# Attention and experts: the router's logits of two tiles at a time taken up later, key and weight transfers asked for one tile sooner

## The chip, the cores and the metric

The kernel runs on one core of a Trainium2 chip. The metric is device time in microseconds (us) from the first to the last instruction of one launch, lower being better; the median of several runs stands for a kernel.

The engines are named as the profile names them: PE is TensorE (matmuls and transposes; PEld are its weight loads, which overlap), DVE is VectorE, ACT is ScalarE, POOL is GpSimd, and SP is the engine from which nearly all transfers (DMAs) are issued. Each engine runs its own list of instructions in order and waits on semaphores for the others.

## The reference

Attention over 4 batches, 8 heads, 768 positions and 64 channels: each query sees the 96 latest positions and 8 global ones. The result is the input of a mixture of 8 experts, each of which takes at most 80 of the tokens whose best logit is its own.

```python
def _attn_ref(q, k, v, n_global, n_local):
    scores = scale * np.matmul(q, k.transpose(0, 1, 3, 2))
    is_global = pos[None, :] < int(n_global)
    is_local = (rel >= 0) & (rel < int(n_local))
    scores = scores - slopes[:, None, None] * dist[None, :, :]
    scores = np.where(is_global | is_local, scores, -1000000000.0)
    a = np.exp(scores - np.max(scores, axis=-1, keepdims=True))
    a = a / (np.sum(a, axis=-1, keepdims=True) + 1e-09)
    return np.matmul(a, v)

def _moe_ref(x, w_gate, w1, w2, capacity):
    logits = x @ w_gate                                   # 3072 x 8
    expert_idx = np.argmax(logits, axis=1)
    gate_w = softmax(logits)[np.arange(N), expert_idx]
    for e in range(E):
        tok_idx = np.where(expert_idx == e)[0]            # the 80 of largest gate_w
        h = np.maximum(x[tok_idx] @ w1[e], 0.0)           # 512 -> 1024
        out[tok_idx] = gate_w[tok_idx, None] * (h @ w2[e])
```

## The kernel before

The 3072 queries are 24 tiles of 128. A tile is two units, u = 2t and 2t + 1, of four heads each; 48 units in all. The main loop (L391 to L424) runs over units and is a software pipeline. In unit u stand, in this order:

- `scores(u)`: PE multiplies queries and keys into PSUM (L181); DVE adds the bias table and takes the row's extreme (L201); ACT takes the exponential and its sum (L205). Between its halves come `transposes(u - 2)`, in which PE turns the weights of two units ago (L242, L250; from u = 20 also a finished tile on its way to DRAM, L255) and ACT copies half of the result to SBUF (L259), and `invert` and `norm` of unit u - 1 (DVE L213, L214; POOL L222).
- `logits2` in every fourth unit: PE transposes the router's logits of two tiles (L330), and DVE reduces them (L359).
- `copied(u - 2)`: DVE copies the other half of the turned weights (L265); from u = 20 the transfer of a finished quarter to `x_dram` (L268) is issued here.
- `logits1` in every fourth unit: PE multiplies two finished tiles by the gate matrix (L318), and DVE copies the product to SBUF (L322).
- `weigh(u - 3)`: PE multiplies weights and values into the one PSUM buffer `pair` (L289, L298). After the second unit of a tile ACT copies `pair` out (L312), and the next tile's first L289 must wait for that copy.
- in even units, SP is asked for the queries of tile u/2 + 2 (`load_q`, 256 KB) and for the next block of keys (`next(keys)`, 272 KB); in odd units for the values of tile u//2 + 1 (two transfers, 208 and 256 KB) and for what `ASKS` names: w is a quarter of an expert's weights (512 KB), o a wipe of a part of the output.
- `routes(n)`: n steps of a generator that finds, group by group (tiles 0 to 5, 6 to 11, 12 to 17, 18 to 21, 22 and 23), each token's expert and gate: small instructions on DVE, POOL and ACT (L505 to L511), comparisons against 127 thresholds (`cf`, L545, DVE), their count by expert on PE (L601), and the rest (L561 onwards; L581 to L588 on POOL). A step may be empty.

The order of PE, DVE, ACT, POOL and SP is the order in which the program is written. Unit 47 and what is left of the pipeline are written out by hand in the string `DRAIN` (L58): its letter r is one routing step, a1 and a2 are `logits1` and `logits2` of tiles 20 and 21, n47 is the last `norm`, t45 to t47 and w44 to w47 are what is left of transposes and weighing. Then a search for each expert's threshold runs, and then the experts' matmuls (L843). A transfer on SP takes one of eight semaphores in turn; a ninth waits until the oldest has landed.

Of the kernel before, what the change touches and what calls it, by code (L numbers as in the profile page):

```python
# [24 lines left out]
NT = B * NB  # L25
# [22 lines left out]
MASK = -8.0e9 * 64  # L48

EARLY = "k12 q1 v0 k23 v1 q2 w0"  # L50
ASKS = "- - w w w w w w w w - o - w - o - w - - w - - -".split()
HELD, EVERY, AHEAD, LATE = 2, 3, 14, 2
FROM, INSIDE = 18, 14
HOLD = 20


DRAIN = (
# [14 lines left out]
def fast_path(tc, a, out, cst, x_dram, inp):  # L72
# [4 lines left out]
    with ExitStack() as ctx:  # L77
# [63 lines left out]
        with tc.tile_pool(name="at_sb", bufs=2) as sp, ExitStack() as sctx:  # L141
# [8 lines left out]
            def idle(n):  # L150
                wake = cst["svx"].rearrange("p s t -> p (s t)")
                for _ in range(n):
                    T.matmul(lps[:, :480], wake[:, :P], wake, start=True, stop=True, skip_group_check=True)

            def begin(u):
                st[u] = [
                    sp.tile([P, 4], F32, tag="nm", bufs=3, name=f"nm{u}"), sp.tile([P, 4], F32, tag="z", bufs=3, name=f"z{u}"),
                    sp.tile([P, 4, WH], F32, tag="ts", name=f"ts{u}"), pwz[u % 3][:, :4 * WH].rearrange("p (j k) -> p j k", j=4),
                ]
# [102 lines left out]
            def copied(u):  # L262
                spot = u - FROM
                ta, tp, n = st[u, "ta"]
                (A.copy if u == nu - 2 else V.tensor_copy)(out=ta[:, 1, :n], in_=tp[:, :n])  # L265
                if 0 <= spot < 2 * INSIDE:
                    r = TURN[spot // 2] * P
                    nc.sync.dma_start(  # L268
                        out=x_dram[r:r + P, :].rearrange("p (i g c) -> p i g c", i=2, g=2)[:, :, spot % 2], in_=ta[:, :, n - P:n])
                st[u, "ta"] = ta  # L270
# [45 lines left out]
            def logits1(t, n):  # L316
                for pr in range(NP):
                    T.matmul(  # L318
                        lps[32 * pr:32 * pr + 32, :n * P], cst["wgn"][:, pr, :], st[t, "ut"][:, pr, :n, :], start=True, stop=True,
                        skip_group_check=True)  # L320
                ls = sp.tile([P, n * P], F32, tag=f"ls{n}", name=f"ls{t}")
                (A.copy if t == NT - 2 else V.tensor_copy)(out=ls, in_=lps[:, :n * P])  # L322
                st[t, "l"] = ls

            def logits2(t, n):

                ls = st.pop((t, "l"))
                if n == 2:
                    for i in range(2):
                        T.transpose(out=part(t + i), in_=ls[:, P * i:P * i + P], identity=ident)  # L330
                else:
                    T.matmul(lgs(t), ls, cst["pick"], start=True, stop=True, skip_group_check=True)
                for i in range(n):
                    collect(t + i)

            def part(t):
                return lps[:, :P] if t % 2 else lps[:, 2 * P:3 * P]

            def lgs(t):
                if t == NT - 1:  # L340

                    if t not in st:
                        st[t] = psa.tile([P, 512], F32, tag="tp0", name="lgl")[:, :E]
                    return st[t]
                if t not in st:
                    st[t] = psa.tile([P, 512], F32, tag="tp1", name="lgk")[:, :E]
                return st[t]

            def collect(t):
                g = next(i for i in range(len(GROUPS)) if t < sum(GROUPS[:i + 1]))  # L350
                n, t0 = GROUPS[g], sum(GROUPS[:g])
                if t == t0:
                    st["rt"] = Route(nc, sp, cst, t0, n)
                rt = st["rt"]
                if n < 3:
                    rt.one(lgs(t), t - t0)
                else:
                    lp = part(t).rearrange("p (q k) -> p k q", q=NP)
                    V.tensor_reduce(out=rt.lg[:, t - t0, :], in_=lp[:, :E, :], axis=AX.X, op=ALU.add)  # L359
                    if t == t0 + n - 1:  # L360
                        routing.append(rt.all())
                        if t0 == 0:
                            routing.append(rt.scale(lps[:, P * NP - 1:]))
                if t == t0 + n - 1:
                    if t < NT - 1:
                        routing.append(rt.rest(lps[:, 3 * P:3 * P + E], cst["capm"]))
# [9 lines left out]
            def routes(n):  # L376
                for _ in range(n):
                    while routing and next(routing[0], END) is END:
                        routing.pop(0)

            routing, cst["later"], cst["landed"] = [], [], []
            nu = 2 * NT
            late = late_constants(nc, a, cst)
            keys = inp.keys(3)
# [6 lines left out]
            for u in range(nu - 1):  # L391
                if u == 0:
                    for _ in cst["first"]:
                        pass
                begin(u)
                scores(u)
                if u % 4 == 1 and 9 <= u:
                    logits2((u - 9) // 2, 2)
                if 2 <= u:
                    copied(u - 2)  # L400
                if u == 1:
                    for _ in window:
                        pass
                    for z in pwz:
                        G.memset(z[:, 4 * WH:], 0.0)
                    G.memset(cst["zero"], 0.0)
                if u > 2:
                    for _ in range(3):
                        next(late, None)
                if u % 4 == 0 and 8 <= u:  # L410
                    logits1((u - 8) // 2, 2)
                if 3 <= u:
                    idle(2 if u == 3 else 0)
                    weigh(u - 3)
                if u % 2 == 0 and 3 <= u // 2 + 2 < NT:
                    inp.load_q(u // 2 + 2, hold=u < HOLD)
                    for _ in range(1 + (u == 20)):
                        next(keys, None)
                if u % 2:
                    if 2 <= u // 2 + 1 < NT:  # L420
                        inp.load_v(u // 2 + 1, hold=u < HOLD)
                    for k in ASKS[u // 2]:
                        next(dict(w=ahead, o=wipe).get(k, iter(())), None)
                routes(5 if u > 40 else 2 + (u % 4 == 3))  # L424
            u = nu - 1
            begin(u)
            scores(u)
# [1 line left out]
            def whole(u):  # L429
                transposes(u)  # L430
                copied(u)

            step = dict(
                w=lambda: next(ahead), o=lambda: next(wipe), t45=lambda: copied(u - 2), t46=lambda: whole(u - 1), t47=lambda: whole(u),
# [957 lines left out]
def build(tc, a, out):  # L1392
    nc = tc.nc
    with tc.tile_pool(name="cst", bufs=1) as cp, tc.tile_pool(name="dr", bufs=1, space=DRAM) as dp:
        x_dram = dp.tile([B * S, DM], F32, name="x_dram")
        lg_dram = dp.tile([B, P, NB, E], F32, name="lg_dram")
        sg_dram = dp.tile([E, P, NT], F32, name="sg_dram")
        cst = Constants(nc, cp)
        late_tiles(cst)
        with tc.tile_pool(name="at_in", bufs=1) as ip:  # L1400
            early = tc.manual_schedule(engines=ORDERED)
            early.__enter__()
            inp = Inputs(nc, a, ip)

            for n, t in (("rel", inp.vb[0]), ("bias", inp.vb[3])):
                cst[n], cst[n + "w"] = t[:, :2 * WH].rearrange("p (h k) -> p h k", h=2), t
            for i, n in enumerate(("r0", "k0", "b0")):
                cst[n] = inp.kt[1].rearrange("p q k -> p (q k)")[:, P * i:P * i + (NG if n == "k0" else P)]
            constants(nc, a, cst)
            inp.more(cst)  # L1410
            early.__exit__(None, None, None)
            fast_path(tc, a, out, cst, x_dram, inp)
            sure = nc.values_load(cst["sure"], min_val=0, max_val=1)
            with tc.If(sure < 1):
                general_path(tc, a, out, cst, x_dram, lg_dram, sg_dram)
# [44 lines left out]
```

## Time and profile before

| | |
|---|---|
| time of three runs, median (lowest, highest) | 257.93 us (257.54, 258.23) |
| time of the profiled execution | 259.51 us |
| span of that execution, first to last instruction | 257.7 us |
| PE, DVE, ACT, POOL busy | 239.6, 213.7, 208.0, 107.5 us |
| granted TensorE clock, mean | 0.977 of full speed |

In the trace the attention takes the span up to 131 us, the drain 131 to 142, the search 142 to 155, the experts 155 to 255. A tile of the attention is told by the starts of its first scores on PE: unit 6 at 20.08 us, unit 8 at 25.16, and so on every 4.6 to 6.9 us; unit 46 starts at 128.04.

A row of the windows gives, for one stretch, its length and then the busy time of PE, PEld, DVE, ACT and POOL (with the number of instructions), the granted clock, the busy share of the 16 DMA engines, and GB/s. A row of a timeline gives start, length, engine, line, operation, output and inputs, the number of instructions run together, and in brackets the idle time before it and what ended that. Where the bracket says "issue", the engine waited for nothing that the profile shows.

### The profile page before, as it was taken

To read this page: it belongs to the slowest core of one execution; us is meant where nothing else is said; L and a number is where in the kernel's file an instruction comes from. 1 tells how busy PE (TensorE), PEld (TensorE's weight loads), DVE (VectorE), ACT (ScalarE), POOL (GpSimd) and SP (SyncE) were. 2 spreads that over 40 slices of the span, in tenths; PEclk is the share of its full clock that TensorE was granted. 3 is DMA by queue.
4 is the path that set the end of the run, shared out by engine and by line. 5 is a ranking of instruction groups with operands and counts; after the bars stand their busy time and mean duration, and the time that the engine had idled before them with its cause. 6 is when DMAs were issued, how large, how long until landed. Compare 5 with 4: busy or idle time off the path is not lost.

```text
span 257.7 us, 9711 instructions
## 1 busy us (share of the span) xinstructions
PE 239.6 (93%) x3587; PEld 169.2 (66%) x3587; DVE 213.7 (83%) x782; ACT 208.0 (81%) x584; POOL 107.5 (42%) x214
## 2 busy tenths in 40 slices
PE   7989998998899999999998798999999999999991
PEld 2567766766677777877667655666666666666660
DVE  3777778987779799898987778999999898999860
ACT  3889899998899999999886636887979898979740
POOL 7667674644445745457470638810000022221111
PEclk9999999999999999999999659999999999999998
DMA  5758999999998999988649976999999999999101
GB/s 145 235 159 218 330 287 280 282 304 300 274 301 247 287 284 316 319 251 230 216 138 311 384 265 204 347 333 401 404 410 408 407 397 398 389 405 364 51 25 36
DMA packets 49086, 73.06 MB, mean 284 GB/s; under 512 B 3688, under 2 KB 23528, under 8 KB 49032
## 3 DMA queue, kind: packets, MB, share of 16 engines
q1 hardware_dynamic: 47864, 69.74, 81.3%
q0 software_dynamic: 1024, 2.62, 3.2%
q8 instruction: 30, 0.49, 0.8%
q14 instruction: 24, 0.20, 0.3%
q10 hardware_dynamic: 144, 0.00, 0.0%
HBM read 58.46 MB, written 13.89 MB: 281 GB/s over the span
## 4 chain that ended last, share of the span: by engine, by line
PE 63%; ACT 13%; DVE 10%; DMA 4%; issue 4%; POOL 3%; SPq 0%; POOLq 0%; DVEq 0%; ACTq 0%
PE hp L843 17%; PE yp L843 17%; ACT pwz L205 9%; PE ring L181 6%; PE pair L289 5%; PE pair L298 3%; DMA kt<-in_kT_dram 3%; PE tp L242 3%; ACT ta L259 2%; DVE ts L201 2%; POOL pwz L222 2%; PE tp L898 2%; PE lps L318 1%; DMA q<-in_q_dram 1%; PE lps L330 1%
## 5 line engine op out<-in xcount | busy, mean ns | idle before, releaser
L205 ACT ACTIVATE pwz<-ts,nm 128x168 f32<-128x168 f32 (+1 forms) x192 | 81.5, 427 | 10.3 <-DVE z L213 6.0
L222 POOL TENSOR_TENSOR pwz<-pwz,z 128x672 f32<-128x672 f32 (+2 forms) x48 | 60.2, 1255 | 53.4 <-DVE z L214 35.5
L201 DVE CUSTOM_DVE_ANT_0 ts<-ring,tab 128x168 f32<-128x168 f32 (+1 forms) x192 | 53.2, 315 | 11.7 <-PE ring L181 11.0
L181 PE MATMUL ring<-kt,q 64*64 64x64 f32 (+3 forms) x1088 | 41.0, 275 | 1.0 <-DMA q<-in_q_dram 0.5
L926 POOL DMA_INDIRECT out_dram<-vb,si x8 | 10.0, 1248 | 76.3 <-ACT xt5h L836 37.9
L205 ACT ACTIVATION_READ_ACCUMULATOR pwz<-ts,nm 128x1 f32 x192 | 36.5, 190 | 0.0
L181 PEld LDWEIGHTS ring<-kt,q 64*64 64x64 f32 x1088 | 32.5, 137 | 4.7 <-issue 2.2
L289 PE MATMUL pair<-ta,va 104*64 104x128 f32 (+1 forms) x368 | 30.5, 285 | 5.1 <-ACT ut L312 3.5
L289 PEld LDWEIGHTS pair<-ta,va 104*64 104x64 f32 (+1 forms) x368 | 19.3, 136 | 14.1 <-issue 7.1
L265 DVE COPY ta<-tp 128x512 f32<-128x512 f32 (+2 forms) x46 | 28.3, 616 | 0.0
L259 ACT COPY ta<-tp 128x512 f32<-128x512 f32 (+2 forms) x47 | 23.8, 507 | 0.5 <-ACT pwz L205 0.5
L242 PE MATMUL tp<-ident,pwz 64*128 64x64 f32 x376 | 21.7, 235 | 1.4 <-POOL pwz L222 0.5
L242 PEld LDWEIGHTS tp<-ident,pwz 64*128 64x128 f32 x376 | 15.3, 138 | 9.1 <-POOL pwz L222 3.5
L817 DVE TENSOR_TENSOR w_3l<-w,w_3h 128x1024 fp32r<-128x1024 f32 x16 | 19.6, 1223 | 1.4 <-ACT w_3h L813 1.3
L817 DVE TENSOR_TENSOR w_0l<-w,w_0h 128x1024 fp32r<-128x1024 f32 x15 | 18.3, 1222 | 2.0 <-ACT w_0h L813 2.0
L298 PE MATMUL pair<-ta,vb 64*64 64x64 f32 x640 | 18.7, 231 | 0.0
L817 DVE TENSOR_TENSOR w_1l<-w,w_1h 128x1024 fp32r<-128x1024 f32 x15 | 18.3, 1220 | 0.0
L817 DVE TENSOR_TENSOR w_2l<-w,w_2h 128x1024 fp32r<-128x1024 f32 x15 | 18.3, 1218 | 0.0
L298 PEld LDWEIGHTS pair<-ta,vb 64*64 64x64 f32 x640 | 13.2, 133 | 6.8 <-issue 6.7
L813 ACT CAST w_3h<-w 128x1024 fp32r<-128x1024 f32 x16 | 16.7, 1045 | 0.3 <-PE yp L843 0.3
L813 ACT CAST w_2h<-w 128x1024 fp32r<-128x1024 f32 x15 | 15.9, 1058 | 1.2 <-PE hp L843 1.0
L201 DVE DVE_READ_ACCUMULATOR2_ANT nm<- 128x1 f32 x192 | 16.0, 83 | 0.0
(441 smaller groups left out, 525.9 us busy)
## 6 DMA issues: line engine op xcount, KB each, us to landing
w<-in_w_dram SPq DMA_DIRECT2D x64, 512.0 KB
kt<-in_kT_dram SPq DMA_DIRECT2D x23, 272.0 KB
out_dram<-zero SPq DMA_DIRECT2D x12, 512.0 KB
q<-in_q_dram SPq DMA_DIRECT2D x23, 256.0 KB
vb<-in_vb_dram SPq DMA_DIRECT2D x20, 256.0 KB
va<-in_va_dram SPq DMA_DIRECT2D x20, 208.0 KB
x_dram<-ta SPq DMA_DIRECT2D x28, 128.0 KB
x_dram<-kt SPq DMA_DIRECT2D x6, 256.0 KB
```

The source lines that it names most:

```text
L181: T.matmul(sc[hh][64 * i:64 * i + 64, pp, o:o + e - c], q[h, pr * P + 64 * i:pr * P + 64 * i + 64], kt[h, pr, c0 + c:c0 + e], start=True, ...
L201: V.tensor_tensor_reduce(out=ts[:, j, :w], in0=sc[hh][:, pp, :w], in1=tab, scale=-0.125, scalar=3.0e38, op0=ALU.add, op1=ALU.min, accum_ou ...
L205: A.activation(out=pw[:, j, :w], in_=ts[:, j, :w], func=AF.Exp, bias=nm[:, j:j + 1], scale=-1.0, accum_out=z[:, j:j + 1],)
L222: eng.tensor_tensor(out=p, in0=p, in1=zs.unsqueeze(2).broadcast_to(list(p.shape)), op=ALU.mult)
L242: T.transpose(out=tps[i][:, 64 * j:64 * j + 64], in_=pw[hs[i], o:o + P], identity=ident[hs[i], hs[i]])
L259: A.copy(out=ta[:, 0, :n], in_=tps[0][:, :n])
L265: (A.copy if u == nu - 2 else V.tensor_copy)(out=ta[:, 1, :n], in_=tp[:, :n])
L289: T.matmul(up[pp][64 * hh:64 * hh + 64], va[:n, 64 * h:64 * h + 64], ta[:n, :, 64 * j:64 * j + 64], start=g == 0 if t < NT - 1 else pp == ...
L298: T.matmul(up[pp][h, 64 * i:64 * i + 64], vb[k, i, 2 * g + pp, :], ta[k, i, 256 + 64 * pp:320 + 64 * pp], start=False, stop=True, skip_gro ...
L813: A.copy(out=hi, in_=src)
L817: V.tensor_tensor(out=lo, in0=src, in1=hi, op=ALU.subtract)
L843: T.matmul(ps, p, q, start=first and i == 0, stop=last and i == 2, skip_group_check=True)
```

## The change

`logits1` of the tile pairs beginning with tiles 0, 2, ... 14 moves from unit 2t + 8 to unit 2t + 9, `logits2` from unit 2t + 9 to 2t + 11; the pairs from tile 16 on stay where they are. The unit with three routing steps is now the one of u % 4 == 0 instead of u % 4 == 3. The second key block that one unit asks for is asked for in unit 4 instead of unit 20, so that every block between is asked for two units sooner. Eight weight quarters are asked for in units 3, 5, ... 17 instead of 5, 7, ... 19. The instructions are the same in kind and number.

```diff
-ASKS = "- - w w w w w w w w - o - w - o - w - - w - - -".split()
+ASKS = "- w w w w w w w w - - o - w - o - w - - w - - -".split()
 HOLD = 20
+SOON = 16
...
+            first = {2 * t + (9 if t < SOON else 8): t for t in range(0, NT - 4, 2)}
+            second = {2 * t + (11 if t < SOON else 9): t for t in range(0, NT - 4, 2)}
...
-                if u % 4 == 1 and 9 <= u:
-                    logits2((u - 9) // 2, 2)
+                if u in second:
+                    logits2(second[u], 2)
...
-                if u % 4 == 0 and 8 <= u:
-                    logits1((u - 8) // 2, 2)
+                if u in first:
+                    logits1(first[u], 2)
...
-                    for _ in range(1 + (u == 20)):
+                    for _ in range(1 + (u == 4)):
                         next(keys, None)
...
-                routes(5 if u > 40 else 2 + (u % 4 == 3))
+                routes(5 if u > 40 else 2 + (u % 4 == 0))
```

On PE, around unit 32 of the kernel before: the transposes to DRAM end, then comes the product of tiles 12 and 13 with the gate matrix (`wgn`), then `weigh` of unit 29 and the scores of unit 33.

```order
891 L255 MATMUL tp_30_2200<-ident,ut_1128 128x64
892 L255 MATMUL tp_30_2201<-ident,ut_1128 128x64
893 L318 MATMUL lps<-ut_1907,wgn 32x256 x4
894 L289 MATMUL pair<-ta_2135,va 64x128 x4
895 L298 MATMUL pair<-ta_2135,vb_118 64x64 x8
896 L181 MATMUL ring_206<-kt_113,q_109 64x104
```

In the changed kernel the same product stands in unit 33, ahead of `weigh` of unit 30 (lines are one to three higher there):

```order
921 L256 MATMUL tp_31_2261<-ident,ut_1132 128x64
922 L256 MATMUL tp_31_2262<-ident,ut_1132 128x64
923 L319 MATMUL lps<-ut_1900,wgn 32x256 x4
924 L290 MATMUL pair<-ta_2197,va 64x128 x4
925 L299 MATMUL pair<-ta_2197,vb_119 64x64 x8
926 L182 MATMUL ring_208<-kt_113,q_110 64x104
```

It moved from a tile's first unit to its second, where L290 is the one that waits for ACT's copy of `pair`.

On SP, units 3 to 5 of the kernel before (values for tile 2, queries and keys for tile 4, values for tile 3, the first weight quarter):

```order
15 L1383 DMA va<-in_va_dram 104x512
16 L1384 DMA vb_118<-in_vb_dram 128x512
17 L1374 DMA q_109<-in_q_dram 128x512
18 L1364 DMA kt_113<-in_kT_dram 128x4x136
19 L1383 DMA va<-in_va_dram 104x512
20 L1384 DMA vb_119<-in_vb_dram 128x512
21 L94 DMA w_0_0_495<-in_w_dram 128x1024
```

and of the changed kernel:

```order
15 L1386 DMA va<-in_va_dram 104x512
16 L1387 DMA vb_118<-in_vb_dram 128x512
17 L95 DMA w_0_0_379<-in_w_dram 128x1024
18 L1377 DMA q_109<-in_q_dram 128x512
19 L1367 DMA kt_113<-in_kT_dram 128x4x136 x2
20 L1386 DMA va<-in_va_dram 104x512
21 L1387 DMA vb_119<-in_vb_dram 128x512
22 L95 DMA w_0_1_499<-in_w_dram 128x1024
```

One weight quarter and one key block more now stand ahead of what units 4 to 20 ask for.

On DVE, unit 45 of the kernel before: the reduction of tiles 18 and 19's logits, the copy of turned weights, and then what follows the count of tiles 12 to 17.

```order
579 L359 TENSOR_REDUCE lg_3131<-lps 128x8 x2
580 L265 COPY ta_3104<-tp_43_3103 128x512
581 L536 TENSOR_TENSOR capm<-capm,lps 127x8
582 L561 TENSOR_SCALAR re<-oh 128x48
583 L562 TENSOR_TENSOR re<-re,sx_2302 128x48
```

The changed kernel has there the last two comparisons that the count needs:

```order
579 L360 TENSOR_REDUCE lg_3129<-lps 128x8 x2
580 L266 COPY ta_3102<-tp_43_3101 128x512
581 L548 TENSOR_TENSOR cf_3076<-sx_2427,kval_65 128x254 x2
582 L202 ISA ts_3160,nm_3158<-ring_208,tab_160 128x128
583 L202 ISA nm_3158 128x1
```

The routing of a group starts two units later, since its logits come two units later, and at the start of the drain eight of its steps are left where four were.

## Rows read from the trace of the kernel before

**Rows 1.** The page, parts 1 and 4: PE's busy time, the chain's shares by engine.
```profile
PE 239.6 (93%) x3587; PEld 169.2 (66%) x3587; DVE 213.7 (83%) x782; ACT 208.0 (81%) x584; POOL 107.5 (42%) x214
PE 63%; ACT 13%; DVE 10%; DMA 4%; issue 4%; POOL 3%; SPq 0%; POOLq 0%; DVEq 0%; ACTq 0%
```
**Rows 2.** Windows by stage: the experts.
```profile
155.00:255.00 100.00, 96.65 (x483) 63.78 (x483) 88.33 (x97) 77.81 (x102) 21.30 (x15) 1.00 0.86 318
```
**Rows 3.** Waits of PE: what it waited for, total us, times, longest.
```profile
PE pair L289 <- ACT ut L312: 3.5, 7, 0.7
...
PE pair L289 <- issue: 1.2, 2, 0.8
...
PE ring L181 <- DMA kt<-in_kT_dram: 0.4, 1, 0.4
```
**Rows 4.** Windows by tile, units 6 to 45, and their sum.
```profile
20.08:25.16 5.08, 4.49 (x135) 3.61 (x125) 3.79 (x23) 4.80 (x20) 3.42 (x12) 1.00 0.81 233
25.16:30.53 5.37, 5.37 (x142) 4.05 (x135) 4.70 (x28) 5.09 (x21) 3.40 (x10) 1.00 1.00 315
30.53:35.58 5.05, 4.56 (x128) 3.68 (x128) 3.75 (x23) 4.61 (x20) 4.15 (x12) 1.00 0.92 282
...
55.98:62.15 6.17, 5.72 (x139) 4.29 (x139) 5.36 (x31) 5.86 (x23) 3.03 (x5) 1.00 1.06 300
62.15:68.08 5.93, 5.10 (x129) 4.04 (x133) 3.76 (x24) 4.20 (x17) 1.91 (x2) 1.00 1.07 318
...
99.92:105.46 5.54, 5.54 (x152) 4.22 (x144) 5.37 (x31) 5.22 (x20) 2.67 (x4) 1.00 0.98 302
105.46:110.62 5.16, 5.16 (x148) 4.33 (x139) 4.12 (x24) 4.94 (x20) 2.46 (x3) 1.00 0.98 320
110.62:116.15 5.53, 5.53 (x151) 4.22 (x143) 5.21 (x30) 5.31 (x21) 3.23 (x4) 1.00 0.84 248
116.15:121.18 5.03, 4.67 (x143) 3.86 (x134) 4.42 (x26) 4.72 (x20) 3.90 (x11) 1.00 0.89 212
121.18:128.04 6.86, 6.24 (x158) 4.76 (x149) 6.22 (x33) 5.73 (x22) 3.08 (x3) 1.00 0.78 259
sum 107.96, PE 101.30 PEld 78.49 DVE 91.92 ACT 99.43 POOL 59.63; mean PE 5.06 PEld 3.92 DVE 4.60 ACT 4.97 POOL 2.98
```
**Rows 5.** Timeline of PE: the end of a tile without logits (unit 7).
```profile
24.29 0.66 PE L289 MATMUL pair<-ta,va 104*64 104x128 f32 x8 [0.46 <-ACT ut L312]
```
**Rows 6.** Timeline of PE, units 44 and 45: logits and count.
```profile
122.61 0.64 PE L318 MATMUL lps<-kt,wgn 128*32 128x256 f32 x8
...
125.62 0.44 PE L330 MATMUL lps<-ident,ls 128*128 128x128 f32 x2
...
127.65 0.46 PE L601 MATMUL lps<-oh,cf 128*127 128x8 bf16 x6 [0.52 <-DVE lg L359]
```
**Rows 7.** Timeline of PE: three waits of units 22 to 25.
```profile
62.15 0.77 PE L181 MATMUL ring<-kt,q 64*64 64x104 f32 x21 [0.45 <-DMA kt<-in_kT_dram]
...
64.85 0.49 PE L289 MATMUL pair<-ta,va 104*64 104x128 f32 x5 [0.83 <-issue]
...
70.48 0.66 PE L289 MATMUL pair<-ta,va 104*64 104x128 f32 x8 [0.37 <-issue]
```
**Rows 8.** Critical chain in order of time: start, us, what; the longest transfer.
```profile
54.22 7.79 DMA kt<-in_kT_dram
```
**Rows 9.** Timeline of SP's queue: keys asked for in unit 4.
```profile
19.07 0.55 SPq L1364 DMA_DIRECT2D kt<-in_kT_dram  x1
```
**Rows 10.** Timeline of DVE, unit 44: routing steps of tiles 12 to 17.
```profile
122.59 0.20 DVE L511 TENSOR_REDUCE sx<-ex 128x6 f32<-128x48 f32 x1 [0.53 <-ACT ex L508]
...
125.03 1.08 DVE L545 TENSOR_TENSOR cf<-sx,kval 128x254 bf16<-128x254 f32 x3
```
**Rows 11.** Timeline of POOL in the drain.
```profile
133.24 0.26 POOL L586 TENSOR_TENSOR bx<-oh,pval 128x48 bf16<-128x48 bf16 x1
...
135.40 0.25 POOL L506 TENSOR_TENSOR ex<-mx,lg 128x32 f32<-128x32 f32 x1 [0.24 <-DVE mx L505]
```

## The prediction

> **What bounds the kernel now.** I read first the page: PE is busy for 239.6 us, 93% of the span, and the chain that ended last lies on PE for 63% and on ACT for 13% [rows 1]. So a gain must come from the 18 us in which PE stands still, or from elsewhere in the chain. The windows by stage leave little of that to the experts, where PE is busy 96.65 of 100 us [rows 2]; they begin when the search ends, and whatever the attention gains or loses shifts them by as much.
>
> The windows by tile say where the attention loses [rows 4]. Over the twenty tiles of units 6 to 45 PE is busy 101.30 of 107.96 us: 6.66 us idle. A tile that carries logits is full: 5.37 us long with PE busy 5.37. A tile without any is not: 5.05 us with 4.56 busy. Such a tile cannot end sooner, since the first `weigh` of the next tile (L289) waits for ACT's copy of `pair` (L312), which stands behind four exponentials, which stand behind that tile's scores; 0.46 us at the end of unit 7 [rows 5], and 3.5 us over seven times in all [rows 3]. That chain takes 5.05 to 5.08 us for a tile, the length of the two tiles without logits. So PE bounds one tile and the chain through ACT the next.
>
> A second loss sits between units 22 and 25. Unit 22 waits 0.45 us for a key block, and twice L289 waits for nothing that the profile shows, 0.83 and 0.37 us [rows 7]: 1.65 us together. The transfer of those keys took 7.79 us [rows 8], and the DMA engines' share there is 1.06 and 1.07, against 0.81 in the first tile of the table [rows 4].
>
> **The move of the logits.** L318 takes 0.64 us and L330 0.44 [rows 6]. Today both stand in the same tile; afterwards each tile has one of them, in its second unit and ahead of the L289 that waits, so that it fills the wait. In the pair of tiles from 25.16 to 35.58 us PE's work becomes 5.37 - 0.44 = 4.93 and 4.56 + 0.44 = 5.00 us, both under the chain's 5.05 to 5.08. The pair takes about 10.13 instead of 10.42 us: 0.29 of its 0.49 idle us come back, 59%. The pair from 99.92 to 110.62 is the opposite: PE is busy for all of its 10.70 us, because its second tile carries the count of tiles 6 to 11. Two units later that count falls into the tile at 110.62, which keeps both logits and has PE busy 5.53 of 5.53. It leaves 0.46 us of room behind and takes the same 0.46 there: no gain, no loss. For the whole I start from the 6.66 us, less the 1.65 above, less the tiles that the move does not reach (0.59 at 20.08, 0.36 at 116.15, 0.62 at 121.18): 3.4 us of idle time. Of that 45%, between the 59% of one pair and the nothing of the other and nearer to the pair that most resemble, is **1.5 us**. A quarter, 0.8, is the low bound, if the chain through ACT is a little longer where transposes to DRAM are added; two thirds, 2.2, the high one.
>
> **Keys and weights asked for sooner.** Of the 1.65 us the 0.45 for keys should go: the block needed in unit 22 will have been asked for in unit 16 instead of 18. Of the two waits marked issue I expect 0.85 of 1.2 back. They lie where the DMA engines are full, and the change takes a weight quarter out of unit 19 and a key block out of unit 20, just ahead of them. Together **1.3 us**, between 0.4 (the keys alone) and 1.65.
>
> Nothing is fetched that was not fetched before, so 512 + 272 = 784 KB now come earlier, about 2.7 us of transfer at the 290 GB/s of a full stretch. The spare is there: the tiles at 20.08 and 30.53 have shares of 0.81 and 0.92 [rows 4]. But the first weight quarter now stands ahead of the queries and keys of unit 4. Those keys are asked for at 19.07 [rows 9] and needed when unit 8 starts, at 25.16, 6.1 us later; a transfer of 512 KB is worth 1.8 us. With the 7.79 us of the full stretch as the far bound they would be 1.7 us late; in a stretch at 0.81 I take a delay of **0.2 us** (0 to 0.4), once.
>
> **The routing.** Its steps cost the same, but each group starts two units later, and only the last full groups run into something. Three comparisons took 1.08 us of DVE in unit 44 [rows 10]. Two of them, 0.72 us, now stand in unit 45 behind the copy of the turned weights, and the count of tiles 12 to 17 on PE needs them; the scores of unit 46 are queued behind that count on PE. The count already waited 0.52 us there [rows 6], in a tile of 6.86 us in which DVE is busy 6.22 [rows 4]. It starts about 1.3 us later in DVE's order (0.72, and the copy), against which DVE loses 0.53 us of waiting for ACT's L508 [rows 10] and has three small steps fewer between count and unit 46. I enter unit 46 0.4 us later (0 to 0.8). In the drain eight steps are left instead of four. Four small ones on POOL, 0.2 to 0.3 us each [rows 11], come behind the last `norm` instead of ahead of it, in front of L506 at 135.40, on which the logits of tiles 18 to 21 hang. That is 0.9 us on POOL, of which I take 0.5 as reaching the end, since the remaining transposes hide part (0.3 to 0.8). Together **0.9 us** (0.3 to 1.6).
>
> **The sum.** -1.5 - 1.3 + 0.2 + 0.9 = -1.7 us. The profiled execution took 259.51 us with a span of 257.7, 1.6 us above the median of the runs; I take the difference over to the median: 257.93 - 1.7 = **256.2 us**. With all terms at their good ends it is 257.93 - 2.2 - 1.65 + 0.3 = 254.4, with all at the bad ends 257.93 - 0.8 - 0.4 + 0.4 + 1.6 = 258.7.
>
> **The rivals.** (1) The early transfers stay ahead of queries and keys, and the kernel is slower. If the 2.7 us of transfer are not absorbed before unit 8 to 22, the queries, which so far have something like a microsecond of room (the keys asked for right behind them come 0.45 us late, and take 0.9 us of transfer), are 1.7 us late somewhere between. Then the gain of 1.3 is gone and half of the 1.5 too: +1.7 - 0.7 + 0.9 = +1.9, 259.8 us. It decides from a loss of 1.6 us in that stretch. Against it speaks the shares of 0.81 and 0.92 in the two tiles without logits there; for it, 1.00 in the first logits tile and 1.06 from 55.98 on [rows 4]. The Trainium skill, "DMA: Bandwidth & Descriptors", section "Queues, rings and completion order", says that on each DMA engine the descriptors of a ring are consumed in ring order; by that rule what SP asks for sooner goes ahead of all that it asks for after, whoever is waiting. No row here contradicts it. 10%.
>
> (2) The transfers move nothing in sum: what the keys no longer wait for, the queries do, and the early tiles, bound by DMA, give nothing back. Then the later half of the logits, 0.7 us, stands against 0.9 of routing: 258.1. For it, the same full shares. 13%.
>
> (3) The late routing costs all it can: eight late steps of 0.3 to 0.4 us, each on the path, 3.2 us. With the gains as forecast it is 257.93 - 2.6 + 3.2 = 258.5. Against it, four of the eight are off DVE and PE. 7%.
>
> (4) The chain through ACT is the floor nearly everywhere, because ACT is busy 5.09 of 5.37 us in a logits tile too [rows 4], and the move gives back 0.5 instead of 1.5: 257.2. 13%.
>
> (5) The routing costs nothing: the count waits in time that the tile has anyway, and the drain hides the POOL steps. 255.3. 17%.
>
> **How the numbers follow.** The forecast has 40%. A measurement of this kernel can tell about 0.3% from no change, 257.16 to 258.70 us. Faster are the forecast, (5) and half of (4): 0.64. Same are (2), (3) and the other half: 0.26. Slower is (1): 0.10. The range reaches from 254.6, a little inside the best sum, to 258.3, past (4) and (2); it leaves out (1), (3) and the best tenth of (5).
>
> **What would show it.** In the changed trace tiles from unit 8 on should be alike in length, 5.1 us early and 5.2 later, where now 5.4 or 5.5 alternates with 5.05; the waits of L289 for L312 should be under 1.5 us in all. Unit 22 should not wait for keys, and the waits marked issue should be under 0.5 us. Up to unit 44 some 3 us should be won, and a third of that lost again by the start of the experts; there the comparisons of unit 45 and L506's successor should be what is waited for. I am wrong if a wait for queries shows up on L181, if L289 still waits for L312 as often, or if the drain is no longer than its 11 us.

## The result: 1.24% slower, where 0.7% faster was forecast

The changed kernel takes 261.43 us (median of five runs, 260.70 to 262.51) against 258.23 for the kernel before beside it (257.54 to 259.72): a ratio of 1.0124, 95% interval 1.0094 to 1.0154. Forecast were 256.2 us and a range of 254.6 to 258.3. Its profiled execution took 260.70 us with a span of 258.9.

The page of the changed kernel, parts 1 and 4, against [rows 1]:

```profile
PE 241.1 (93%) x3587; PEld 171.0 (66%) x3587; DVE 213.6 (83%) x782; ACT 206.8 (80%) x584; POOL 103.3 (40%) x214
PE 58%; ACT 17%; DVE 14%; issue 4%; POOL 4%; POOLq 0%; DVEq 0%; ACTq 0%
```

PE's share of the chain falls from 63% to 58%, DVE's rises from 10% to 14%; PE is busy 1.5 us longer with the same instructions, because its clock is lower for longer. Waits of PE in the changed kernel, against [rows 3]:

```profile
PE pair L290 <- ACT ut L313: 1.4, 3, 0.6
...
PE jb L669 <- DVE gs L465: 0.7, 1, 0.7
PE lps L604 <- DVE cf L548: 0.7, 1, 0.7
```

The wait for ACT's copy of `pair` fell from 3.5 to 1.4 us, as foreseen. New is the wait of the count (L604) for the comparisons (`cf`); the wait of the search's first step (L669) for the end of the routing is 0.7 us, where the kernel before has 0.3. Windows by tile of the changed kernel, first the two tiles of units 8 to 11, then that of units 40 and 41, against [rows 4]:

```profile
25.10:30.13 5.03, 5.00 (x132) 3.78 (x132) 3.60 (x23) 4.22 (x19) 2.63 (x9) 1.00 1.05 303
30.13:36.24 6.11, 5.16 (x134) 3.98 (x129) 4.69 (x27) 5.79 (x24) 5.28 (x16) 1.00 0.92 301
...
107.96:114.48 6.52, 6.11 (x157) 4.77 (x149) 5.03 (x29) 5.43 (x20) 2.89 (x3) 1.00 0.78 228
```

The first tile is 5.03 us as forecast; the second loses 0.75 us to a wait marked issue, in the timeline of PE:

```profile
36.11 0.27 PE L299 MATMUL pair<-ta,vb 64*64 64x64 f32 x2 [0.75 <-issue]
```

The tile of unit 40, which now carries both logits and the count, takes 6.52 us where [rows 4] has 5.53.

Where the loss is made late is seen in unit 45. The timeline of PE there (start, length, operation, idle before):

```profile
125.42 0.22 PE L604 MATMUL lps<-oh,cf 128*127 128x8 bf16 x2 [0.20 <-DVE lg L360]
126.34 0.61 PE L604 MATMUL lps<-oh,cf 128*127 128x8 bf16 x4 [0.71 <-DVE cf L548]
126.89 0.67 PE L182 MATMUL ring<-kt,q 64*64 64x128 f32 x16
...
128.12 0.98 PE L290 MATMUL pair<-ta,va 104*64 104x128 f32 x8
...
129.52 1.08 PE L182 MATMUL ring<-kt,q 64*64 64x128 f32 x16
```

and of DVE:

```profile
125.28 0.68 DVE L266 COPY ta<-tp 128x512 f32<-128x512 f32 x1
125.88 0.75 DVE L548 TENSOR_TENSOR cf<-sx,kval 128x254 bf16<-128x254 f32 x2
```

The count waits 0.91 us, 0.71 of it for the two comparisons behind DVE's copy; it waited 0.52 us before [rows 6]. Then something new follows: L290 takes 0.98 us instead of 0.66, the scores 1.08 instead of 0.67. The granted clock fell. Windows of the changed kernel (the third number from the end is the granted clock):

```profile
122.00:128.00 6.00, 5.04 (x124) 4.04 (x120) 4.94 (x27) 4.17 (x17) 2.07 (x2) 1.00 0.58 164
128.40:131.60 3.20, 3.20 (x60) 2.42 (x56) 2.81 (x19) 2.79 (x13) 1.46 (x2) 0.50 0.30 104
```

From 128.4 to 131.6 us PE runs at half clock (1.2 GHz instead of 2.4) though it is busy for all of it; what came before is the unit in which it stood for 0.91 us. In the drain the four small POOL steps come behind the last `norm` and ahead of L509, the successor of L506 in [rows 11], as the prediction had it:

```profile
134.49 0.22 POOL L588 CAST bx<-og 128x48 bf16<-128x48 f32 x1
...
135.30 0.24 POOL L509 TENSOR_TENSOR ex<-mx,lg 128x32 f32<-128x32 f32 x1
```

### The profile page after: what moved, and what is told of

Read it like the earlier page. It is cut to its first block, busy times and chain, and to the rows that moved or that the text cites. A ratio compares the mean times of both kernels' runs of the same rounds, so it can differ in the third digit from the quotient of the medians.

```text
span 258.9 us, 9711 instructions
## 1 busy us (share of the span) xinstructions
PE 241.1 (93%) x3587; PEld 171.0 (66%) x3587; DVE 213.6 (83%) x782; ACT 206.8 (80%) x584; POOL 103.3 (40%) x214
## 4 chain that ended last, share of the span: by engine, by line
PE 58%; ACT 17%; DVE 14%; issue 4%; POOL 4%; POOLq 0%; DVEq 0%; ACTq 0%
PE hp L846 17%; PE yp L846 17%; ACT pwz L206 12%; PE ring L182 4%; PE pair L290 4%; DVE ts L202 4%; ACT ta L260 3%; PE pair L299 3%; PE tp L243 2%; DVE ta L266 2%; PE tp L901 2%; PE lps L319 2%; ACT ut L313 2%; POOL pwz L223 2%; PE lps L597 1%
## 5 line engine op out<-in xcount | busy, mean ns | idle before, releaser
L290 PE MATMUL pair<-ta,va 104*64 104x128 f32 (+1 forms) x368 | 30.6, 288 | 2.2 <-ACT ut L313 1.4
L290 PEld LDWEIGHTS pair<-ta,va 104*64 104x64 f32 (+1 forms) x368 | 19.3, 137 | 11.2 <-ACT ut L313 7.3
L243 PEld LDWEIGHTS tp<-ident,pwz 64*128 64x128 f32 x376 | 15.7, 139 | 10.0 <-POOL pwz L223 4.5
L299 PE MATMUL pair<-ta,vb 64*64 64x64 f32 x640 | 19.3, 233 | 1.1 <-issue 1.1
```

What stands on the lines that cost most here:

```text
L243: T.transpose(out=tps[i][:, 64 * j:64 * j + 64], in_=pw[hs[i], o:o + P], identity=ident[hs[i], hs[i]])
L290: T.matmul(up[pp][64 * hh:64 * hh + 64], va[:n, 64 * h:64 * h + 64], ta[:n, :, 64 * j:64 * j + 64], start=g == 0 if t < NT - 1 else pp == ...
L299: T.matmul(up[pp][h, 64 * i:64 * i + 64], vb[k, i, 2 * g + pp, :], ta[k, i, 256 + 64 * pp:320 + 64 * pp], start=False, stop=True, skip_gro ...
```

## Experiments

All ratios are against the kernel before on the same chip. In the diffs `routes` stands for the loop's last line.

**The routing caught up, and the parts apart.** First the whole change with the third routing step back in the units of u % 4 == 3, and four steps more in units 31 to 34:

```diff
-                routes(5 if u > 40 else 2 + (u % 4 == 0))
+                routes(5 if u > 40 else 2 + (u % 4 == 3) + (31 <= u < 35))
```

> The whole change, with the routing caught up: three steps instead of two in units 31 to 34 (and the third step back in units of u % 4 == 3), so that the groups of tiles 6 to 11 and 12 to 17 and the drain stand as in the kernel before. Theory A, the late routing costs: in the trace of the changed kernel unit 39 starts 3.2 us earlier than before and the first expert matmul 0.8 later, so 4.0 us are lost in between (a count behind unit 40, one behind unit 45, the clock that falls after it, a longer low clock in the search). All of it should come back: 257.4 us (256.5 to 258.3), with the clock at 1.00 up to 142 us. Theory B, the early transfers cost: the routing moves under 1 us and the time stays at 260.5 to 261.5.

1.0045 (1.0015 to 1.0075). About 2 us of the 3.2 are back; the clock holds until the search, and the count of unit 45 waits as it did before. But the kernel is not faster than before: theory A has some two thirds of the loss and not the rest.

Only the logits and the routing steps, keys and `ASKS` as before:

```diff
-ASKS = "- w w w w w w w w - - o - w - o - w - - w - - -".split()
+ASKS = "- - w w w w w w w w - o - w - o - w - - w - - -".split()
...
-                    for _ in range(1 + (u == 4)):
+                    for _ in range(1 + (u == 20)):
```

> Only the logits and the routing steps moved; keys and weights are asked for as in the kernel before. Theory A: the late routing is all there, and the gain of the transfers in units 20 to 25 is not: 260.5 to 262 us, with the fall of the clock behind unit 45. Theory B: 257 to 258 us.

1.0113 (1.0070 to 1.0157): without the transfers the loss is as large, as far as the intervals tell. The opposite, only keys and weights sooner:

```diff
-ASKS = "- - w w w w w w w w - o - w - o - w - - w - - -".split()
+ASKS = "- w w w w w w w w - - o - w - o - w - - w - - -".split()
...
-                    for _ in range(1 + (u == 20)):
+                    for _ in range(1 + (u == 4)):
```

> Only the key block and the eight weight quarters asked for sooner; logits and routing as before. Theory A: no lag, the waits of units 22 to 25 gone (1.65 us), a delay of unit 8 to 14: 256 to 258 us. Theory B: 260 to 261 us.

1.0024 (0.9987 to 1.0061): no gain can be measured, and one above 0.13% (0.3 us) is excluded; 1.1 us net were forecast for this part. And the logits with the routing caught up, both edits of the first two runs:

> The logits moved and the routing caught up by unit 35; keys and weights as before. Theory A: the gain of the logits alone, up to 1.5 us as predicted: 256.7 to 258.2 us, faster than the logits alone by 2 to 4 us. Theory B: like the logits alone, within 0.8 us.

1.0039 (1.0012 to 1.0065), 0.74% better than with the lag. The late routing costs 0.7 to 0.8% with the early transfers and without them. Both catch-ups also move the third routing step to other units, so this is the price of the two together.

**Which part of the lag.** The catch-up after unit 40, so that the count of tiles 6 to 11 stays behind unit 40:

```diff
-                routes(5 if u > 40 else 2 + (u % 4 == 0))
+                routes(6 if 41 <= u < 45 else 5 if u > 40 else 2 + (u % 4 == 0))
```

> The whole change, with one routing step more in each of units 41 to 44: the count of tiles 6 to 11 stays behind unit 40, but that of tiles 12 to 17 and the drain stand as in the kernel before. Theory A, unit 45, the fall of the clock after it and the drain are what the late routing costs: within 0.8 us of the catch-up by unit 35, 258.5 to 260 us, clock at 1.00 through 126 to 134 us. Theory E, the count behind unit 40 (0.97 us in the trace) is half of it: 260 to 261.

1.0050 (1.0014 to 1.0087), as good as the early catch-up. Unit 45, the clock behind it and the drain, which this edit puts back, are the 0.74% between 1.0124 and 1.0050: 1.9 us. In its trace unit 46 starts 6.86 us after unit 44 and unit 47 2.11 us after unit 46, as in the kernel before.

That the tile of 6.52 us costs nothing does not follow, for the two catch-ups also differ in the place of the third step. In the traces units 38 to 41 take 11.67 us here and 11.66 in the changed kernel, against 10.69 in the kernel before [rows 4] and 11.06 with the early catch-up where no transfer is waited for (the logits spread in the light kernel, below). Units 16 to 37 take 57.20 us here and 57.79 there. So the late count costs some 0.6 us against the early catch-up, and the other place of the third step has given as much back before.

Whether it is the clock alone: five matmuls on constants in unit 45, ahead of the count.

```diff
+                if u == 45:
+                    wake = cst["svx"].rearrange("p s t -> p (s t)")
+                    for _ in range(5):
+                        T.matmul(ring[2][:, :480], wake[:, :P], wake, start=True, stop=True, skip_group_check=True)
                 routes(5 if u > 40 else 2 + (u % 4 == 0))
```

> The whole change as it is, with five matmuls on constants put ahead of the count in unit 45, into a score buffer that is free there (0.2 us each at full clock), so that PE is busy while it waits there. The late routing itself stays. Theory H, the fall of the clock behind unit 45 (3.4 us at half speed) is half or more of the 2 us that the late routing costs: 259.5 to 260.7 us against 261 to 261.5, faster than the change by 0.8 to 1.5, clock at 1.00 from 126 to 134 us. Theory I, the waits of the late routing are all of it: within 0.5 us of the change.

1.0094 (1.0055 to 1.0132), between the theories; the interval overlaps with that of the change. Its profiled execution took 265.42 us, 4.5 above the median of its runs, so only its units 45 to 47 are read. Timeline of PE:

```profile
130.95 1.19 PE L430 MATMUL ring<-svx 128*128 128x480 bf16 x5
131.97 0.78 PE L608 MATMUL lps<-oh,cf 128*127 128x8 bf16 x6
132.69 0.67 PE L182 MATMUL ring<-kt,q 64*64 64x128 f32 x16
...
134.80 0.62 PE L182 MATMUL ring<-kt,q 64*64 64x128 f32 x16
```

PE has no idle time ahead of the count, and unit 47 starts 2.11 us after unit 46, with scores of 0.62 us, where the changed kernel has 129.52 - 126.89 = 2.63 and 1.08. Filling the wait kept the clock in this execution; three traces with the late count and without the filling (the change, the logits alone, the change without its later queries) all have the fall behind unit 45. The length of a wait alone does not decide: ahead of unit 40 PE stood 1.38 us for keys in this trace and 1.43 us in that of the logits alone, and the granted clock stayed at 1.00. What the clock is worth in the end, by the times some 0.8 us, is not measured sharply.

**Was the wait for keys in the kernel at all?** The kernel before, twice more, unchanged.

> The kernel before, unchanged, for a second profile. Theory C, the 1.65 us of waits in units 22 to 25 belong to that one execution (259.51 us, 1.8 above the median of 25 runs): here they are under 0.6 us and the span is 255.5 to 256.5. Theory D, they belong to the kernel: 1.2 to 2 us again.

263.0 us. Its PE waits are larger and partly elsewhere. Timeline of PE:

```profile
71.07 0.66 PE L289 MATMUL pair<-ta,va 104*64 104x128 f32 x8 [1.22 <-issue]
102.01 0.86 PE L181 MATMUL ring<-kt,q 64*64 64x104 f32 x24 [1.31 <-issue]
```

> The kernel before, unchanged, a third profile (the first took 259.51 us, the second 263.0). Theory C: what its execution takes over 257.5 us is about the sum of PE's waits for transfers and of those marked issue in units 6 to 47 (1.65 us in the first, about 4 in the second); in an execution near the median of 258 they are under 0.6 us. Theory D: such waits are there in an execution near the median too, over 1.2 us.

257.11 us, and these are all the waits of PE that the view names between 14 and 131 us:

```profile
PE pair L289 <- ACT ut L312: 3.5, 7, 0.7
PE lps L601 <- DVE lg L359: 0.5, 1, 0.5
PE pair L289 <- ACT kt L312: 0.4, 1, 0.4
PE lps L318 <- ACT kt L312: 0.2, 1, 0.2
PE tp L242 <- POOL pwz L222: 0.2, 1, 0.2
PE lps L330 <- DVE ls L322: 0.2, 1, 0.2
```

No transfer and no issue among them, while the waits for L312 are those of [rows 3]. Its windows by tile for units 20 to 23, against 6.17 and 5.93 in [rows 4]:

```profile
55.06:60.60 5.54, 5.54 (x152) 4.22 (x143) 5.18 (x31) 5.26 (x21) 2.90 (x5) 1.00 1.02 316
60.60:65.62 5.02, 4.90 (x142) 4.01 (x137) 4.26 (x25) 4.72 (x20) 2.39 (x3) 1.00 0.99 293
```

The share of the DMA engines is nearly the same, and PE waits for no transfer. So the waits of [rows 7] are not in every execution of the kernel. But the execution without them is 1.55 us below the median of the 29 runs beside it (258.66), the one with them 1.3 above the median of 258.23 of the result: none at the median was profiled, and how much of these waits an ordinary execution has is not shown. The second profile had 4.2 us of them in units 9 to 36, not the 0.6 of theory C; 0.9 us more of its time lie in the search, whose stretch at half clock lasts 13.7 us in it and 10.2 in the first and third.

**What the spread of the logits gives when transfers are out of the way.** Queries not loaded from tile 10 on, in the kernel before and in the logits with the routing caught up:

```diff
     def load_q(self, t, ks=slice(0, NP * P), hold=False):
+        if t >= 10:
+            return
```

> The kernel before without the loads of queries from tile 10 on (256 KB of about 990 KB for a tile); the queries of four tiles earlier stand in their place, so the result differs. It is the base for the next run. The transfers should no longer be waited for in units 20 to 47. Theory F, the attention runs close to what the DMA engines give: faster than before by 0.5 to 2 us. Otherwise within 0.5 us.

> The logits moved and the routing caught up by unit 35, keys and weights as before, and the queries not loaded from tile 10 on, as in the run beside it. Theory F, the spread of the logits gains its 1.0 to 1.5 us on the engines and loses it to transfers: here faster than the light kernel before by 0.8 to 1.8 us. Theory G, the spread gains nothing on the engines: within 0.5 us of the light kernel before, or slower.

0.9990 (0.9968 to 1.0012) and 0.9969 (0.9945 to 0.9992). So taking a quarter of a tile's transfers out of the kernel before, from tile 10 on, gains nothing measurable. The spread gains 0.2% on that by the ratios, 0.5 us with intervals that overlap, and 0.1 us by the medians (257.75 and 257.66): not 0.8 us. Neither trace has a wait for a transfer in units 8 to 43, so here the two orders can be compared. The sums of nine windows by pair of tiles, units 8 to 43, first the light kernel before:

```profile
sum 93.75, PE 89.92 PEld 69.67 DVE 81.87 ACT 88.45 POOL 53.08; mean PE 9.99 PEld 7.74 DVE 9.10 ACT 9.83 POOL 5.90
```

then with the logits spread:

```profile
sum 94.00, PE 90.18 PEld 69.79 DVE 81.30 ACT 88.09 POOL 53.10; mean PE 10.02 PEld 7.75 DVE 9.03 ACT 9.79 POOL 5.90
```

In this order nothing is gained. Waits of PE from 24 to 108 us, light kernel before (waits of 0.3 us in all and more):

```profile
PE pair L289 <- ACT ut L312: 2.9, 6, 0.7
```

and with the logits spread:

```profile
PE tp L243 <- POOL pwz L223: 1.2, 5, 0.3
PE pair L290 <- ACT ut L313: 0.8, 2, 0.5
PE tp L243 <- ACT pwz L206: 0.6, 1, 0.6
PE lps L604 <- DVE lg L360: 0.3, 1, 0.3
```

The wait for the copy of `pair` goes, and PE waits for the normalized weights instead. Behind that, ACT waits more for DVE, the light kernel before:

```profile
ACT pwz L205 <- DVE z L213: 2.3, 7, 0.5
ACT pwz L205 <- DVE nm L201: 1.5, 7, 0.3
```

with the logits spread:

```profile
ACT pwz L206 <- DVE z L214: 3.1, 7, 0.7
ACT pwz L206 <- DVE nm L202: 1.8, 9, 0.2
```

ACT is busy 88 of 94 us, and its waits for DVE grow from 3.8 to 4.9 us: the small DVE instructions of the logits (L323, L360) and of the routing now stand at other places ahead of what feeds the exponentials. That they are the reason was not tried apart. The place of the third routing step has a part in it: units 20 to 27 take 21.3 us in this trace and in both catch-ups by unit 35 with all transfers, and 20.5 in the changed kernel, which has that step in other units; the light kernel before takes 20.6.

**One half of the logits only, or one unit less of lag.** The second half moved by two units, the first left where it was (routing caught up by unit 35, transfers as before):

```diff
-            first = {2 * t + (9 if t < SOON else 8): t for t in range(0, NT - 4, 2)}
+            first = {2 * t + 8: t for t in range(0, NT - 4, 2)}
```

> Only the second half of the logits (the transposes L330 and the reductions L359) moved by two units, the first half where it was, the routing caught up by unit 35, keys and weights as before. Theory J, it is the first half in the odd unit (L318, and the copy L322 on DVE at the border of two tiles) that costs 1 us with all transfers: within 0.4 us of the kernel before. Theory K, any spread costs it, since the tiles then ask for transfers more evenly sooner: slower than before by 0.6 to 1.4 us.

0.9996 (0.9962 to 1.0029). Then the halves in units 2t + 9 and 2t + 10, caught up by unit 33:

```diff
-            second = {2 * t + (11 if t < SOON else 9): t for t in range(0, NT - 4, 2)}
+            second = {2 * t + (10 if t < SOON else 9): t for t in range(0, NT - 4, 2)}
```

> The first half of the logits in unit 2t + 9 as in the change, the second in 2t + 10 (the changed kernel has 2t + 11), the routing caught up by unit 33, keys and weights as before: each tile still has one of them, one unit after the other. Theory J: slower than before by 0.5 to 1.4 us, as the logits moved with the routing caught up (1.0). Theory L, what cost there was the second half beside the count of unit 38: within 0.4 us of before or faster.

1.0008 (0.9967 to 1.0050). Both are level with before. The first of them leaves theory K only the low end of its range (0.29% is 0.75 us), the second does not exclude it; between J and L the intervals do not decide, for they overlap with the 1.0039 of the first arrangement.

**The rest of the loss.** The whole change without the later queries, and the odd-even order with the early transfers.

> The whole change as it is, without the loads of queries from tile 10 on (those of four tiles earlier stand in their place, so the result differs). Theory M, the late routing costs its 2 us whatever the transfers do, and the rest of the loss (about 1 us) is waits for transfers that come with the spread logits: 259 to 260 us, 0.4 to 0.8% above the kernel before, with the same 0.9 us of waits in unit 45, the fall of the clock and a drain of 11.1 to 11.2 us. Theory N, the late routing alone accounts for all of it: 1.0 to 1.3% above.

1.0157 (1.0106 to 1.0208), no better than the change with all transfers. Theory M's 0.4 to 0.8% falls: the later queries' transfers are not the rest. Waits as such are not ruled out, for its trace still has 0.60 us for keys ahead of unit 40. It shows the same fall of the clock, and two waits in units 9 and 11, before the edit sets in. Timeline of PE:

```profile
30.57 0.34 PE L299 MATMUL pair<-ta,vb 64*64 64x64 f32 x6 [0.55 <-issue]
36.15 0.27 PE L299 MATMUL pair<-ta,vb 64*64 64x64 f32 x2 [0.30 <-issue]
```

> The first half of the logits in unit 2t + 9, the second in 2t + 10, the routing caught up by unit 33, and keys and weights asked for sooner as in the change: the parts of the change with the lag taken out as far as the runs so far show. Theory M, none of the parts gains anything in an ordinary execution: within 0.5% of the kernel before, on either side. Theory P, the transfers asked for sooner take away waits that the spread logits bring: 0.3 to 0.6% faster than before.

1.0057 (1.0027 to 1.0087): theory P falls, and the early transfers do not help where they could. Beside the 1.0008 without them they look harmful, but the run with the whole change caught up (1.0045) and its twin without the transfers (1.0039) do not say so. No version here that loads all its queries is faster than the kernel before.

## Why the prediction was wrong, step by step

The two gains of the sum, 2.8 us together, did not come, and the late routing cost twice what it was entered with.

**Keys and weights, 1.3 us forecast, nothing measured.** This step failed first of all in its method. The waits of [rows 7] were taken from an execution of 259.51 us and the gain subtracted from a median of 257.93. The difference of 1.6 us was noticed and "taken over"; it is the size of those waits. The execution at 257.11 us has none of them, the light kernel before is level with the full one, and the early transfers alone measure 1.0024. Units 20 to 27, where the waits stood, take 20.56 us with the early transfers and 20.56 in the execution at 257.11: there is nothing left there for earlier keys to win. What an execution does not wait for cannot be won in it.

**The logits, 1.5 us forecast, about 0.7 won and 0.9 lost again.** The wait for L312 went as described (3.5 to 1.4 us), and the first tile with a half of the logits came out at 5.03 us. Windows of units 6 to 15, 16 to 37 and 38 to 41 in the execution of the kernel before that waits for no transfer (257.11 us):

```profile
19.44:44.80 25.36, 23.15 (x594) 17.66 (x584) 20.38 (x120) 23.55 (x94) 16.36 (x51) 1.00 0.90 288
44.80:102.47 57.67, 55.77 (x1390) 43.12 (x1388) 51.55 (x295) 54.76 (x214) 30.65 (x41) 1.00 0.97 299
102.47:113.22 10.75, 10.75 (x285) 8.59 (x277) 9.35 (x54) 10.31 (x39) 5.72 (x6) 1.00 0.92 271
```

and in the changed kernel:

```profile
19.41:45.62 26.21, 23.76 (x594) 18.06 (x584) 20.32 (x118) 23.35 (x94) 16.34 (x51) 1.00 0.97 299
45.62:102.82 57.20, 55.91 (x1388) 43.13 (x1387) 50.12 (x290) 54.32 (x214) 30.62 (x40) 1.00 0.95 288
102.82:114.48 11.66, 11.21 (x287) 8.82 (x279) 10.10 (x57) 10.25 (x39) 5.35 (x5) 1.00 0.88 258
```

Units 16 to 37, where neither waits for a transfer, gain 0.47 us (57.67 also in the light kernel before, 57.20 and 57.22 in the catch-up after unit 40 and the change without its later queries); with the third routing step in its old units the spread alone gains nothing there (57.79, above). Units 6 to 15 gain 0.19 in the trace of the logits alone (25.17 us). That is a fifth of the 3.4 us of idle time, where 45% were booked. What failed is the floor: 5.05 us, read off one short tile without logits, was taken to hold for all tiles, and the idle time of PE as what could come back. In the light pair PE's idle time is 3.8 us before and after. The fourth rival, that ACT's chain is the floor nearly everywhere and 0.5 us come back, was nearest in size; it was given 13%.

The other part that failed is the count of tiles 6 to 11, entered as "no gain, no loss": units 38 to 41 take 0.91 us more. PE was busy there all the time before. The room that the count leaves in the tile of units 38 and 39 is taken by the half of the logits that moves there (L331, 0.44 us), and in unit 40 the count waits 0.41 us for DVE.

**The routing, 0.9 us forecast, about 2 measured** (1.0124 against 1.0045 and 1.0050; 1.0113 against 1.0039). The places were the right ones: unit 45, and the POOL steps ahead of L509. Unit 46 starts 0.53 us late by it (0.4 forecast): it is 7.39 us behind unit 44 where the kernel before has 6.86. From unit 47 to the search's first transposes the drain takes 140.72 - 129.52 = 11.20 us where the kernel before takes 10.4, 0.8 more (0.5 forecast). Missing altogether was the clock: unit 46 takes 2.63 us where it took 2.11. The step counted how long PE waits, and not that what comes after may run slower. These three make 1.9 us. With the 0.91 us of units 38 to 41 the late routing costs 2.8 us, near the 3.2 of the third rival, which had 7%.

**The early delay, 0.2 us forecast, 0.85 in the trace.** Units 7 and 11 lose 0.32 and 0.75 us to waits marked issue in the changed kernel, and units 6 to 15 take 26.21 us instead of 25.36. A wait of 0.81 us marked issue also stands in unit 9 of the logits caught up without the early transfers, so it is not the first weight quarter alone that does it, as the step assumed. But from unit 6 to unit 8 all six traces with the early transfers and moved logits take 5.42 to 6.73 us, and the ten others 5.07 or 5.08. With the early transfers alone no wait is named there, yet units 8 to 11 take 10.75 us where the execution at 257.11 takes 10.29. The trace of the change has no wait for queries in units 8 to 22, and with it the first rival's mechanism falls. The rule of ring order that the prediction took from the Trainium skill ("DMA: Bandwidth & Descriptors", "Queues, rings and completion order") is not contradicted by that: what was asked for sooner may well have gone ahead, but in the run of the transfers alone no wait of PE for a transfer is named in units 4 to 22.

**Where the rest lies, and what stays open.** Of the 3.2 us, 1.9 are unit 45, the clock and the drain. The traces place the rest, by one execution each: the span of the changed kernel is 3.6 us above that of the execution at 257.11. Units 38 to 41 make 0.9 of the other 1.7, units 6 to 15 0.85, the search 0.5, and 0.5 are won in units 16 to 37. The search's part need not be the change's doing: its stretch at half clock, 13.7 us in the changed kernel, lasts 10.2, 13.7 and 10.2 us in the three executions of the kernel before.

Waits for transfers and waits marked issue differ from one execution to the next: each trace of a kernel with moved logits and all transfers has 0.8 us or more of them in units 6 to 47, but so have two of three executions of the kernel before, and the light run of the change kept its loss and 1.6 us of such waits. What those marked issue are, the transfers in the traces suggest. The queue marked instruction brings packets of 16 KB, some 4 to 11 us apart. Of 25 waits marked issue in units 7 to 39 of eleven traces, 24 end 1.2 to 1.6 us after such a packet has ended, one 2.4 us after. In the changed kernel the packet before the wait of unit 11 ends at 34.86, and PE goes on at 36.11. The row of that queue, window 33.6 to 34.9 (packets, MB, share of the time of the 16 DMA engines):

```profile
q8 instruction: 1, 0.02, 6.0%
```

So PE then most likely waits for its own next instructions, whose packets are counted on the same DMA engines as the data. No run tested it.

Slower was given 10%, for late queries, which the trace does not show.

## What to carry to other kernels

When the profiled execution is slower than the median by more than a step is worth, profile once more before a wait is counted as a gain: a wait that moves or vanishes between executions of the same kernel cannot be booked as a gain. An idle engine in a pipeline of four is an upper bound on the gain only; take the next engine's busy share (here ACT's 94%) as the floor before the difference is booked. And work that is put later at one end has to be followed to the other: the steps left over at the end cost 1.9 us, more than the whole spread gave.

## What the hardware showed

Waits of 0.91 us in one unit were followed by over 3 us at half the granted clock, in the next two units, while PE was busy for all of them (0.50 in the window from 128.4 to 131.6 us). Five matmuls in that gap kept the clock at 1.00 in the run that has them. Single waits of 1.38 and 1.43 us ahead of unit 40 left it at 1.00 (the run with the five matmuls, the logits alone), and one of 2.19 us in unit 9 of the former was followed by 3.4 us at half clock. The stretch at half clock in the search lasted 10.2 or 13.7 us in executions of one and the same kernel, and the search took 14.6, 14.7 or 15.7 us from its first count to the first expert matmul. A DMA share of 1.06 came with 0.45 us of waiting for keys in one execution, and one of 1.02 in the same tile with none in another.
